# Natural channel order for the second pair's tables, GpSimd costs in the plan, and a new instruction order, in a state-space convolution with an MLP

## The chip, the cores and the metric

The kernel runs on one core of one Trainium2 chip. The metric is device microseconds of one execution of the whole program, less being better. Each engine (TensorE = PE, its weight loads = PEld, VectorE = DVE, ScalarE = ACT, GpSimd = POOL, and SyncE = SP, which issues the DMAs) works through its own instructions in order and waits on semaphores for the others.

## The reference

A pre-norm block over 2048 positions of 512 channels: a diagonal state-space model (S4) as a long convolution, then a channel MLP.

```python
def _A_ref(u, A_re, A_im, B_re, B_im, C_re, C_im, log_dt, Dskip):
    dt = jnp.exp(log_dt)[:, None]
    logdA = dt * (A_re + 1j * A_im)               # 512 x 128
    dB = dt * (B_re + 1j * B_im)
    P = jnp.exp(logdA[:, :, None] * l[None, None, :])
    K = jnp.einsum("dn,dnl,dn->dl", Cc, P, dB).real
    Kf, Uf = rfft of K and u, padded to 4096
    y = irfft(Uf * Kf)[..., :L]
    return y + u * Dskip

def _B_ref(x, w1, b1, w2, b2):
    h = gelu(layernorm(x) @ w1 + b1)              # 512 -> 1376
    return h @ w2 + b2

h = x + _A_ref(layernorm(x), ...)
h2 = h + _B_ref(layernorm(h), ...)
```

## The kernel before

The 512 channels are four blocks c = 0..3 of 128, in two pairs: hf or q = 0 is the first pair (c = 0, 1), 1 the second (c = 2, 3). The kernel K(d, l) of a channel is a product over the 128 states of two tables: A with `NA` = 20 rows and B with `NB` = 33 rows, so that A times B, summed over the states, gives the values at all needed positions l. Each table has a real part and an imaginary part of the complex exponential, so per channel there are two small matmuls that add up.

The stages, in the order of the data:

- *Start.* DMAs bring A, B, C, log_dt (as `raw` and `ldt`) and the input u; TensorE transposes A_re with an identity matrix that GpSimd builds (`ident_fn`, L649); VectorE multiplies it with dt into `th` (the decay rates of the channels). GpSimd also fills field tables with many one-column memsets (`fld_fn` L667, `ca_fn` L719). Splits into a high and a low half and `restack`, many small SBUF-to-SBUF DMAs issued by SyncE (L549), bring rates and phases into the layout in which TensorE multiplies them by positions. ScalarE scales two of the splits (`split`, `CP`, L606); both engines are allowed.
- *Magnitudes.* `bexps` (ScalarE, L774) writes the B tables `EB`, `aexps` (TensorE L985, ScalarE L989 for the first pair and L992 for the second) the A tables `EA` (c = 0, 1) and `EA2` (c = 2, 3).
- *Phases.* `chain(hf, kind)` adds phase steps in PSUM by matmuls (L1033, L1036, L1042), takes a Sin and a Cos of them (ScalarE, L1051, 1024 entries each) into one of three scratch buffers `SC`, and VectorE multiplies the magnitudes by them into imaginary tables (`IA`, `IB`, `IA2`) and real tables in place: with one instruction of 2048 entries (`product`, L1012), or, for the second pair's B tables, with two of 1024 (L1070, L1071).
- *Products.* `kgen(c)` multiplies, channel by channel: 128 channels, four at a time in the four column quarters of the array, each with one matmul of the real tables (L1101) and one of the imaginary (L1102), 20 stationary columns and 33 moving ones. Results are cast from PSUM, Dskip is added to one row (L1115), and `carry` (L1122) moves rows by DMA.
- *Spectrum.* `kspec` (TensorE L1145) transforms K to frequencies in two halves of rows and two blocks; the casts go to SBUF, by DMA to DRAM (`AK_d`) and back in another layout, and `fstage` (L959) does the second step of the transform. `xspec` (L939, L959) does the same for the normalised input (`unorm`, L927, on VectorE or GpSimd; its statistics L915).
- *Back.* `inverse` multiplies the spectra (L1193; VectorE or GpSimd), transforms back (L1209), turns by DMA transposes (L1215); `tail` (L1272 to L1315) adds x, takes the second layer norm, whose reciprocal root GpSimd computes as a power (`root`, L895; VectorE continues at L614), and `mlp` (L1331 to L1355) does the two MLP matmuls, the GELU (L1333) and the residual, and stores.

Casts from PSUM (`evac`) go to ScalarE (L537) or VectorE (L539). PSUM is four buffers of two banks, handed out by the scheduler. L1447 are TensorE instructions without use that fill gaps.

In `chain` and `aexps`, channels of the first pair keep their natural order: entry d of a block at element d of a 128-entry row, so a channel's 20 A entries lie 256 bytes apart. The second pair's A tables are stored by quarter g, row a, channel i (`EA2`, `IA2`: shape (2, 4, 32, 32)), so the 20 entries of a channel lie 64 bytes apart; its B tables hold channel 32g + i at element 4i + g:

```python
if c < 2:
    Ar, Ai = EA[c], IA[c]
    w, x = (lambda v, g, i: v.ap()[:, :, 32 * g + i]), (lambda v, g, i: v.ap()[:, :, 32 * g + i])
else:
    Ar, Ai = EA2[c - 2], IA2[c - 2]
    w, x = (lambda v, g, i: v.ap()[:, g, 0:NA, i]), (lambda v, g, i: v.ap()[:, :, 4 * i + g])
...
pe.matmul(o, lhsT=w(Ar, g, i0 + i), rhs=x(Br, g, i0 + i), start=True, stop=False, tile_position=(0, 32 * g))
pe.matmul(o, lhsT=w(Ai, g, i0 + i), rhs=x(Bi, g, i0 + i), start=False, stop=True, tile_position=(0, 32 * g))
```

All work is a list of 982 steps (`S.add`), each with its engine or engines and a cost in microseconds, and their data dependencies. `ORDER` is a written list of all steps: it sets the order on every engine, the engine where there are two (a negative entry takes the second), and, over a model of the costs (`Sched.run`), which PSUM buffer a step gets and how many filling matmuls go in. A GpSimd step also waits for the VectorE step last issued before it. The model's costs have no other effect on the program.

Of the kernel before, what the change touches and what calls it, by code (L numbers as in the profile page):

```python
# [9 lines left out]
ACT = mybir.ActivationFunctionType  # L10
# [152 lines left out]
class VS(V):  # L163
# [49 lines left out]
]  # L213


FREE = {"PE": 5.0, "ACT": 0.7, "DVE": 0.8, "POOL": 1.4, "SP": 0.7}
WIN, PHASE, ACTIVE = 3.4133, -1.4, 1.25
SWITCH = 0.095


class Clock:
    def __init__(self):
        self.end, self.act, self.warm = PHASE + WIN, 0.0, False

# [184 lines left out]
def kernel(ctx, tc, A_u, A_A_re, A_A_im, A_B_re, A_B_im, A_C_re, A_C_im, A_log_dt, A_Dskip,  # L409
# [64 lines left out]
    EB0 = E0 + 2 * ASZ  # L474
    BA0 = E0 + 2 * ASZ + NCH * BSZ
    IB0 = BA0 + 2 * ASZ
    IA2 = at(BA0 + 2 * ASZ + NCH * BSZ, bf16, 2, 4, 32, 32)
    EA2 = at(IA2.hi, bf16, 2, 4, 32, 32)
    pos[0] = EA2.hi
    HF = 2 * ASZ + 2 * BSZ  # L480
# [1013 lines left out]
```

## Time and profile before

| | us |
|---|---|
| median of 3 runs | 246.31 (246.04 to 247.08) |
| the profiled execution | 247.44 |
| its span, first to last instruction | 245.6 |
| TensorE busy | 208.3 (85%) |
| VectorE busy | 179.9 (73%) |
| ScalarE busy | 182.8 (74%) |
| GpSimd busy | 48.1 (20%) |

The granted TensorE clock was 1.0. In the profile, a row of the timeline gives start and duration in us, engine, line, operation, operands, count, and in brackets how long the engine had been idle and what released it; a row of groups gives busy us, mean ns of one, and idle time before. Busy time of TensorE counts overlapping matmuls once.

### The profile page before, as it was taken

The page shows a single profiled execution, that of the slowest core. Times are in us where ns is not written, and L with a number is a line of the kernel's source. Part 1 is how long each engine was busy: PE and PEld are TensorE (multiplying, and loading weights), DVE is VectorE, ACT ScalarE, POOL GpSimd, SP SyncE. Part 2 cuts the span into 40 slices and gives each one's busy share as a digit, 9 for nine tenths or more (in the row PEclk, how much of TensorE's full clock was granted, in tenths as well). Part 3 has the DMA queues.
Part 4 walks back from the last instruction along what each step waited for, and adds up shares of the span by engine and source line. Part 5 has one row for each costly group of instructions (what it writes and reads, how often), then busy time and mean ns, then how long its engine had stood idle before and what let it go on. Part 6 is the DMA issues. An engine that isn't in the chain of part 4 may idle for free.

```text
span 245.6 us, 7723 instructions
## 1 busy us (share of the span) xinstructions
PE 208.3 (85%) x3268; PEld 116.5 (47%) x3279; DVE 179.9 (73%) x311; ACT 182.8 (74%) x215; POOL 48.1 (20%) x225
## 2 busy tenths in 40 slices
PE   7200788867999999999699898999999999999994
PEld 3200543323776697645576434554444444444452
DVE  0999958899999996489886888999980887031021
ACT  4999998999999987889798979999356214704600
POOL 8834431000000041234604271010000001000000
PEclk9999999999999999999999999999999999999999
DMA  4293250100000160499868958307845053410303
GB/s 150 53 205 76 71 99 17 43 4 3 3 5 5 34 174 7 118 276 275 339 113 155 230 170 286 91 3 138 122 85 109 0 96 86 77 33 21 85 17 79
DMA packets 42755, 24.28 MB, mean 99 GB/s; under 512 B 26145, under 2 KB 40066, under 8 KB 42722
## 3 DMA queue, kind: packets, MB, share of 16 engines
q1 hardware_dynamic: 42130, 23.34, 39.8%
q8 instruction: 25, 0.41, 0.7%
q10 hardware_dynamic: 592, 0.46, 0.6%
q14 instruction: 8, 0.07, 0.1%
HBM read 10.03 MB, written 6.29 MB: 66 GB/s over the span
## 4 chain that ended last, share of the span: by engine, by line
PE 38%; DVE 8%; DMA 4%; ACT 3%; issue 2%; POOL 1%; SPq 0%; DVEq 0%; POOLq 0%
PE ps L1331 15%; PE ps L1353 14%; PE ps L1209 4%; ACT ar L537 3%; DMA AK_d<-ar 2%; DVE ar L1287 2%; DMA ar<-AK_d 2%; PE ps L959 2%; DVE ar L539 1%; PE ps L1277 1%; PE ps L939 1%; DVE ar L1193 1%; POOL ar L895 1%; DVE ar L1284 1%; DVE ar L1198 0%
## 5 line engine op out<-in xcount | busy, mean ns | idle before, releaser
L537 ACT CAST ar<-ps 128x1024 bf16<-128x1024 f32 (+2 forms) x71 | 67.6, 1025 | 15.2 <-DMA ar<-ar 3.5
L1333 ACT ACTIVATE ar<-ps,ar 128x512 bf16<-128x512 f32 (+1 forms) x44 | 29.0, 693 | 25.0 <-PE ps L1331 23.6
L1331 PE MATMUL ps<-ar 128*128 128x512 bf16 (+1 forms) x176 | 39.9, 379 | 0.0
L1353 PE MATMUL ps<-ar 128*128 128x512 bf16 (+3 forms) x181 | 39.2, 366 | 0.6 <-DVE ar L1355 0.3
L1051 ACT ACTIVATE ar<-ps 128x1024 bf16<-128x1024 int16 x36 | 34.6, 1051 | 2.6 <-PE ps L1042 0.9
L1355 DVE TENSOR_TENSOR ar<-ps,ar 128x512 bf16<-128x512 f32 (+1 forms) x17 | 11.0, 656 | 27.8 <-PE ps L1353 20.0
L539 DVE CAST ar<-ps 128x1024 bf16<-128x1024 f32 (+1 forms) x21 | 23.9, 1151 | 5.2 <-PE ps L959 2.8
L1353 PEld LDWEIGHTS <-ar 128*128 128x128 bf16 (+1 forms) x187 | 18.0, 98 | 20.4 <-issue 1.0
L1193 DVE TENSOR_TENSOR ar<-ar 128x2048 bf16<-128x2048 bf16 x22 | 26.5, 1228 | 1.2 <-PE ps L1209 0.9
L1331 PEld LDWEIGHTS <-ar 128*128 128x128 bf16 (+1 forms) x176 | 17.2, 100 | 20.1 <-issue 0.8
L1042 PE MATMUL ps<-ar 128*32 128x512 f16 (+1 forms) x368 | 21.9, 331 | 4.8 <-ACT ar L1051 3.6
L1101 PE MATMUL ps<-ar 128*20 128x33 bf16 x512 | 24.4, 277 | 0.8 <-issue 0.5
L1102 PE MATMUL ps<-ar 128*20 128x33 bf16 x512 | 24.5, 279 | 0.0
L985 PE MATMUL ps<-ar 128*32 128x256 f16 x160 | 7.3, 341 | 19.1 <-DVE ar L722 18.4
L1101 PEld LDWEIGHTS <-ar 128*20 128x20 bf16 x512 | 22.0, 135 | 2.7 <-issue 1.0
L1102 PEld LDWEIGHTS <-ar 128*20 128x20 bf16 x512 | 22.2, 136 | 1.4 <-issue 0.9
L895 POOL TENSOR_TENSOR ar<-ar 128x4 f32<-128x4 f32 (+1 forms) x5 | 5.8, 1165 | 67.6 <-DVE ar L588 44.6
L959 PE MATMUL ps<-ar 128*32 128x256 bf16 (+1 forms) x384 | 17.4, 309 | 1.4 <-DMA ar<-AK_d 1.0
L621 ACT ACTIVATE ar<-ar 128x512 f32<-128x512 f32 (+9 forms) x19 | 16.2, 864 | 3.0 <-DMA ar<-in_A_log_dt_dram 2.9
L1012 DVE TENSOR_TENSOR ar<-ar 128x2048 bf16<-128x2048 bf16 x14 | 16.9, 1219 | 0.3 <-ACT ar L1051 0.2
L939 PE MATMUL ps<-ar 128*32 128x512 bf16 x256 | 16.7, 381 | 0.0
L1042 PEld LDWEIGHTS <-ar 128*32 128x32 f16 x368 | 9.5, 97 | 14.5 <-issue 10.8
(104 smaller groups left out, 305.0 us busy)
## 6 DMA issues: line engine op xcount, KB each, us to landing
AK_d<-ar SPq DMA_DIRECT2D x8, 512.0 KB
ar<-AK_d SPq DMA_DIRECT2D x8, 512.0 KB
ar<-in_A_u_dram SPq DMA_DIRECT2D x4, 512.0 KB
out_dram<-ar SPq DMA_DIRECT2D x30, 64.0 KB
ar<-in_B_w_dram SPq DMA_DIRECT2D x4, 344.0 KB
ar<-ar SPq DMA_DIRECT2D x40, 32.0 KB
ar<-in_B_w_dram SPq DMA_DIRECT2D x2, 640.0 KB
ar<-ar SPq DMA_DIRECT2D x8, 48.0 KB
```

Source lines behind the costliest of these rows:

```text
L537: act.copy(out_fn(), in_fn())
L539: dve.tensor_copy(out_fn(), in_fn())
L939: pe.matmul(pst(p)[32 * cg:32 * cg + 32, 512 * z:512 * z + 512], lhsT=BD.ap()[:, 32 * f + 2 - 2 * jl:32 * f + 34 - 2 * jl], rhs=un[2 * (2 ...
L959: pe.matmul(pst(p)[64 * h + z:64 * h + z + 32, w * (k + r):w * (k + r) + w], lhsT=T.ap()[:, f, r, z:z + 32], rhs=rhs(f), start=True, stop= ...
L1042: pe.matmul(pst(p)[32 * g:32 * g + 32, 256 * j:256 * (j + n)].rearrange("p (a b) -> p a b", a=n), lhsT=W2[DELTAS.index(d)].ap(), rhs=S2[g] ...
L1051: add("ACT", c_act(1024), lambda e, o_=o_, i_=i_: act.activation(o_(), i_(), ACT.Sin, scale=SINSC), r=[p, TBL], w=[sc[cs]])
L1101: pe.matmul(o, lhsT=w(Ar, g, i0 + i), rhs=x(Br, g, i0 + i), start=True, stop=False, tile_position=(0, 32 * g))
L1102: pe.matmul(o, lhsT=w(Ai, g, i0 + i), rhs=x(Bi, g, i0 + i), start=False, stop=True, tile_position=(0, 32 * g))
L1193: (dve if e == "DVE" else gp).tensor_tensor(pieces(o).rearrange("p z (a r d) -> p a z r d", a=4, r=2), k, x, ALU.mult)
L1331: pe.matmul(pst(p)[:fs, 512 * z:512 * z + 512], lhsT=w1s[dc].ap()[:, fc * P:fc * P + fs], rhs=ybuf.ap().rearrange("p (t c) k -> p c t k", ...
L1333: add("ACT", c_act(512, 1), lambda e, p=p, z=z, fc=fc, fs=fs: act.activation(hT.ap()[:fs, fc, :], pst(p)[:fs, 512 * z:512 * z + 512], ACT. ...
L1353: pe.matmul(pst(p)[:, 512 * z + c0:512 * z + c1], lhsT=hT.ap()[:fs, fc, 128 * t:128 * t + 128], rhs=w2s[fc].ap()[:fs, c0:c1], start=(fc == ...
```

## The change

The second pair's tables take the first pair's layout. `th` loses its permuted copy, so three multiplications become one. `EA2` and `IA2` stay where they were and become plain addresses of two tables of 20 x 128 each; `aexps`, `chain` and `kgen` treat both pairs alike. In `chain` the second pair's two B products per group become one `product`, and its A products write rows of 512 entries where they wrote runs of 128. The sines of the second pair's B tables are no longer permuted. The GpSimd costs of `root`, `unorm` and `inverse` in the plan are changed. `ORDER` is new: 976 steps, with 43 on GpSimd (50 before), 310 on VectorE (310), 221 on ScalarE (220), 273 on TensorE (273) and 129 on SyncE (129).

What the new order does, where the prediction speaks of it:

- On GpSimd, the identity follows an iota, the field memsets (`fld_fn`), an iota, `ca_fn` and an iota; before, it was the third step.
- The two scalings of the phase splits (`CP` in `split`) go from ScalarE to VectorE; eight small memsets and three larger steps go from GpSimd to VectorE, and three from VectorE to GpSimd; of the first half's eight `unorm` steps GpSimd takes six (before three, one of which moves to VectorE), and of the second half's eight, six (before eight).
- On SyncE, the four loads of u stand earlier among the `restack` DMAs, one piece of w2 (`w2s[10]`) stands among them, and a bias load goes behind them. After the first pair's carries come three writes to `AK_d`, the two reads of the first of these, and then the second pair's carries.
- On TensorE, the second pair's products hold two `kspec` steps: the first pair's block 0, upper rows, after the first 32 groups of four channels' matmuls, and block 1, upper rows, after 76 of 128.
- On ScalarE, after the last Sin of `chain`: four `kspec` casts, the Sin over 2048 entries (`T`), a `kspec` cast, the table load for the GELU, the first cast of the second pair's products.
- On VectorE, two casts stand between the operand of the 8-entry `root` and the step that reads its result.

```diff
 ORDER = [
...
-    IA2 = at(BA0 + 2 * ASZ + NCH * BSZ, bf16, 2, 4, 32, 32)
-    EA2 = at(IA2.hi, bf16, 2, 4, 32, 32)
-    pos[0] = EA2.hi
+    IA2 = BA0 + 2 * ASZ + NCH * BSZ
+    EA2 = IA2 + 16384
+    pos[0] = EA2 + 16384
...
-    EA = [at(E0 + c * ASZ, bf16, NA, CW) for c in range(2)]
+    EA = [at(lo + c * ASZ, bf16, NA, CW) for lo in (E0, EA2) for c in range(2)]
...
-    IA = [at(BA0 + c * ASZ, bf16, NA, CW) for c in range(2)]
+    IA = [at(lo + c * ASZ, bf16, NA, CW) for lo in (BA0, IA2) for c in range(2)]
...
-    th = tL(f32, 5, 256)
+    th = tL(f32, 4, 256)
     p, pa = tr("are")
-    TT(th[2], p, dtb, ALU.mult, n=256, psum=True, oap=by4(th[2], 0, 256), aap=lambda pa=pa: pa()[:, 0:64], bap=by4(dtb, 0, 256))
-    def th3(e, p=p):
...
-    add("DVE", c_dve(256, 1, True), th3, r=[p, dtb], w=[th[3]], hv=0)
-    TT(th[4], p, dtb, ALU.mult, n=256, psum=True, oap=by4(th[4], 0, 256), aap=lambda pa=pa: pa()[:, 64:128], bap=by4(dtb, 256, 512), pr=0.42)
+    TT(th[2:4], p, dtb, ALU.mult, psum=True, oap=lambda: th[2:4].ap().rearrange("p h d -> p (h d)").rearrange("p (q d) -> p q d", d=4), aap=pa, bap=by4(dtb))
...
-        add("POOL", 0.3, lambda e: gp.tensor_tensor(y.ap(), v_.ap(), mhalf.ap()[:, 0:n], ALU.pow), r=[v_, mhalf], w=[y], hv=6, pr=pr)
+        add("POOL", 0.4 + 0.16 * n, lambda e: gp.tensor_tensor(y.ap(), v_.ap(), mhalf.ap()[:, 0:n], ALU.pow), r=[v_, mhalf], w=[y], hv=6, pr=pr)
...
-            add(("DVE", "POOL"), (c_dve(512, 4) + 0.13, 0.6), ufn, hv=9, r=[hs[8 * b + j], nw[b][3], nw[b][4]], w=[un[j]], pr=pr + 0.001 * (j // 4))
+            add(("DVE", "POOL"), (c_dve(512, 4) + 0.13, 1.15), ufn, hv=9, r=[hs[8 * b + j], nw[b][3], nw[b][4]], w=[un[j]], pr=pr + 0.001 * (j // 4))
...
-                if hf == 0:
-                    add("ACT", c_act(1024), lambda e, p=p, n=n: act.activation(multi(E0 + 4 * n * 256, ASZ, bf16, 2, 4, CW).rearrange("p c a d -> p a c d"), pst(p).rearrange("p (a c d) -> p a c d", a=4, c=2), ACT.Exp),
-                        r=[p, TBL], w=[EA[c][4 * n + z] for c in range(2) for z in range(4)])
-                else:
-                    add("ACT", c_act(1024), lambda e, p=p, n=n: act.activation(dmaj(EA2, 4 * n).rearrange("p x a i -> p a x i"), pst(p).rearrange("p (a x i) -> p a x i", a=4, x=8), ACT.Exp),
-                        r=[p, TBL], w=[EA2])
+                e0 = (E0, EA2)[hf]
+                add("ACT", c_act(1024), lambda e, p=p, n=n, e0=e0: act.activation(multi(e0 + 4 * n * 256, ASZ, bf16, 2, 4, CW).rearrange("p c a d -> p a c d"), pst(p).rearrange("p (a c d) -> p a c d", a=4, c=2), ACT.Exp),
+                    r=[p, TBL], w=[EA[2 * hf + c][4 * n + z] for c in range(2) for z in range(4)])
...
-                if dm:
-                    o_, i_ = (lambda sc=sc, cs=cs: sc[cs].ap().rearrange("p a d -> p (a d)").rearrange("p (x a i) -> p a x i", x=8, a=4)), (lambda p=p: i16v(p).rearrange("p (a x i) -> p a x i", a=4, x=8))
-                elif hf:
-                    o_, i_ = (lambda sc=sc, cs=cs: ced(sc[cs]).rearrange("p c e (i g) -> p e c i g", g=4)), (lambda p=p: i16v(p).rearrange("p (e c g i) -> p e c i g", c=2, g=4, i=32))
-                else:
-                    o_, i_ = (lambda sc=sc, cs=cs: ced(sc[cs]).rearrange("p c e d -> p e c d")), (lambda p=p: i16v(p).rearrange("p (e c d) -> p e c d", e=4, c=2))
+                o_, i_ = (lambda sc=sc, cs=cs: ced(sc[cs]).rearrange("p c e d -> p e c d")), (lambda p=p: i16v(p).rearrange("p (e c d) -> p e c d", e=4, c=2))
...
-            if dm:
-                out = (lambda b0=b0: V(ar, IA2.lo, bf16, (2, 8, 1024)).ap()[:, :, :, 32 * b0:32 * b0 + 128])
-                product(out, lambda o: o[:, 1], sc, [EA2, sc], [IA2, EA2] + mark)
-                continue
...
-                e0, i0, q, lo = E0, BA0, ASZ, b0 * 256
+                e0, i0, q, lo = (E0, EA2)[hf], (BA0, IA2)[hf], ASZ, b0 * 256
             rE, rI = regs(e0, q, lo, 4), regs(i0, q, lo, 4)
-            if hf:
-                add("DVE", c_dve(1024, 2), lambda e, lo=lo, Sx=Sx, e0=e0, i0=i0, q=q: dve.tensor_tensor(ent(i0, q, lo, 4), ent(e0, q, lo, 4), Sx(), ALU.mult), r=rE + [sc[0]], w=rI)
-                add("DVE", c_dve(1024, 2), lambda e, lo=lo, Cx=Cx, e0=e0, q=q: dve.tensor_tensor(ent(e0, q, lo, 4), ent(e0, q, lo, 4), Cx(), ALU.mult), r=rE + [sc[1]], w=rE + mark)
-                continue
             product(lambda e0=e0, q=q, lo=lo: both(e0, q, lo, 4), lambda o: o[:, 1], sc, rE + [sc], rE + rI + mark)
...
-        Br, Bi = EB[c], IB[c]
...
+        Ar, Br, Ai, Bi = EA[c], EB[c], IA[c], IB[c]
...
-                                pe.matmul(o, lhsT=w(Ar, g, i0 + i), rhs=x(Br, g, i0 + i), start=True, stop=False, tile_position=(0, 32 * g))
-                                pe.matmul(o, lhsT=w(Ai, g, i0 + i), rhs=x(Bi, g, i0 + i), start=False, stop=True, tile_position=(0, 32 * g))
+                                pe.matmul(o, lhsT=Ar.ap()[:, :, d], rhs=Br.ap()[:, :, d], start=True, stop=False, tile_position=(0, 32 * g))
+                                pe.matmul(o, lhsT=Ai.ap()[:, :, d], rhs=Bi.ap()[:, :, d], start=False, stop=True, tile_position=(0, 32 * g))
...
-                add(("DVE", "POOL"), (c_dve(2048, 2), 4.85), mul, hv=5, r=[kf[f0:f0 + 8], X.h[f0 // 8][c]], w=o)
+                add(("DVE", "POOL"), (c_dve(2048, 2), 4.0), mul, hv=5, r=[kf[f0:f0 + 8], X.h[f0 // 8][c]], w=o)
```

More of the change, by code (lines that the diff above doesn't have):

```diff
@@ L502 @@
     OB = [[PR[0:2], PR[2:4]], [QR, [at(lo + 24576, bf16, 4, 2, CW) for lo in (E0, BA0)], [at(sc0 + 12288 + 2048 * n, bf16, 4, 2, CW) for n in range(2)]]]
-    Z = [[at(lo, bf16, P, 16) for lo in q] for q in ((zlo, sc0 + 8192), (EA2.lo + 11264, IA2.lo + 11264))]
+    Z = [[at(lo, bf16, P, 16) for lo in q] for q in ((zlo, sc0 + 8192), (EA2 + 11264, IA2 + 11264))]
     assert pos[0] <= NBYTES, pos[0]
-    EA = [at(E0 + c * ASZ, bf16, NA, CW) for c in range(2)]
+    EA = [at(lo + c * ASZ, bf16, NA, CW) for lo in (E0, EA2) for c in range(2)]
     EB = [at(EB0 + c * BSZ, bf16, NB, CW) for c in range(NCH)]
-    IA = [at(BA0 + c * ASZ, bf16, NA, CW) for c in range(2)]
+    IA = [at(lo + c * ASZ, bf16, NA, CW) for lo in (BA0, IA2) for c in range(2)]
     IB = [at(IB0 + c * BSZ, bf16, NB, CW) for c in range(NCH)]
@@ L566 @@
     tE = Tmp(BA0, BA0 + HF)
-    tL = Tmp(BA0 + HF, IA2.hi)
+    tL = Tmp(BA0 + HF, EA2)
     ct = tL
@@ L756, in tr @@
         return p, (lambda: nat(pst(p, bf16)[:, 0:512]))
-    th = tL(f32, 5, 256)
-    thn = lambda: th.ap().rearrange("p h d -> p (h d)").rearrange("p (a q) -> p a q", q=256)[:, 2:5:2, :]
+    th = tL(f32, 4, 256)
     p, pa = tr("are")
-    TT(th[2], p, dtb, ALU.mult, n=256, psum=True, oap=by4(th[2], 0, 256), aap=lambda pa=pa: pa()[:, 0:64], bap=by4(dtb, 0, 256))
-    def th3(e, p=p):
-        for c in range(2):
-            o = th[3].ap().rearrange("p (c e d g) -> p c e d g", c=2, e=8, d=4)[:, c]
-            x = pst(p, bf16)[:, 0:512].rearrange("p (d c g e) -> p c e d g", d=4, c=4, g=4)[:, 2 + c]
-            y = dtb.ap().rearrange("p (c g e d) -> p c e d g", c=4, g=4, e=8)[:, 2 + c]
-            dve.tensor_tensor(o, x, y, ALU.mult)
-    add("DVE", c_dve(256, 1, True), th3, r=[p, dtb], w=[th[3]], hv=0)
-    TT(th[4], p, dtb, ALU.mult, n=256, psum=True, oap=by4(th[4], 0, 256), aap=lambda pa=pa: pa()[:, 64:128], bap=by4(dtb, 256, 512), pr=0.42)
+    TT(th[2:4], p, dtb, ALU.mult, psum=True, oap=lambda: th[2:4].ap().rearrange("p h d -> p (h d)").rearrange("p (q d) -> p q d", d=4), aap=pa, bap=by4(dtb))
     CP(th[0:2], th[2:4], -1.0, n=512, pr=0.35)
@@ L807 @@
     STT(lnd, lnd, 2.0, s1, ALU.mult, ALU.add)
+    thn = lambda: th[2:4].ap().rearrange("p h d -> p (h d)")
     HLt = tL(f16, 2, 512)
@@ L811 @@
     TT(HLg[1], lnd, HLg[0], ALU.subtract, pr=0.41, eng="POOL")
-    TS(HLt[0], th[2:5], 1.0, None, ALU.mult, iap=thn, oap=lambda: HLt[0].ap().rearrange("p (a q) -> p a q", q=256), pr=0.42)
-    STT(HLt[1], th[2:5], 1.0, HLt[0], ALU.mult, ALU.subtract, aap=thn, oap=lambda: HLt[1].ap().rearrange("p (a q) -> p a q", q=256), bap=lambda: HLt[0].ap().rearrange("p (a q) -> p a q", q=256), pr=0.42)
+    TS(HLt[0], th[2:4], 1.0, None, ALU.mult, iap=thn, pr=0.42)
+    STT(HLt[1], th[2:4], 1.0, HLt[0], ALU.mult, ALU.subtract, aap=thn, pr=0.42)
     S3 = tL(f16, 4, 512)
@@ L971, in regs @@
         return [at(lo0 + q * c + lo, bf16, n, CW) for c in range(2)]
-    def dmaj(v, a):
-        return v.ap().rearrange("p c g a i -> p (c g) a i")[:, :, a:a + 4, :]
     def aexps(pr):
@@ L1000, in both @@
     def both(lo0, q, lo, n):
-        k = BA0 - E0
-        a = ar[:, E0 // 2:E0 // 2 + k].rearrange("p (z q) -> p z q", z=2)[:, ::-1, (lo0 - E0) // 2:(lo0 - E0) // 2 + q]
+        if lo0 == EA2:
+            a = ar[:, IA2 // 2:IA2 // 2 + 16384].rearrange("p (z q) -> p z q", z=2)[:, :, 0:q]
+        else:
+            k = BA0 - E0
+            a = ar[:, E0 // 2:E0 // 2 + k].rearrange("p (z q) -> p z q", z=2)[:, ::-1, (lo0 - E0) // 2:(lo0 - E0) // 2 + q]
         return a.rearrange("p z (c q) -> p z c q", c=2)[:, :, :, lo // 2:lo // 2 + n * CW]
@@ L1015, in chain @@
     def chain(hf, kind, pr):
-        dm = hf == 1 and kind == "A"
         ch0 = 256 * hf
@@ L1080, in kgen @@
     def kgen(c, pr):
-        Br, Bi = EB[c], IB[c]
-        if c < 2:
-            Ar, Ai = EA[c], IA[c]
-            w, x = (lambda v, g, i: v.ap()[:, :, 32 * g + i]), (lambda v, g, i: v.ap()[:, :, 32 * g + i])
-        else:
-            Ar, Ai = EA2[c - 2], IA2[c - 2]
-            w, x = (lambda v, g, i: v.ap()[:, g, 0:NA, i]), (lambda v, g, i: v.ap()[:, :, 4 * i + g])
+        Ar, Br, Ai, Bi = EA[c], EB[c], IA[c], IB[c]
         kg = Kg[c // 2]
@@ L1099, in fn @@
                             for g in range(4):
+                                d = 32 * g + i0 + i
                                 o = pst(p)[32 * g:32 * g + NA, 512 * nb:512 * nb + NB * n].rearrange("p (k i) -> p k i", i=n)[:, :, i]
-                                pe.matmul(o, lhsT=w(Ar, g, i0 + i), rhs=x(Br, g, i0 + i), start=True, stop=False, tile_position=(0, 32 * g))
-                                pe.matmul(o, lhsT=w(Ai, g, i0 + i), rhs=x(Bi, g, i0 + i), start=False, stop=True, tile_position=(0, 32 * g))
+                                pe.matmul(o, lhsT=Ar.ap()[:, :, d], rhs=Br.ap()[:, :, d], start=True, stop=False, tile_position=(0, 32 * g))
+                                pe.matmul(o, lhsT=Ai.ap()[:, :, d], rhs=Bi.ap()[:, :, d], start=False, stop=True, tile_position=(0, 32 * g))
                     add("PE", 0.14 * (hi - lo), fn, r=[Ar, Br, Ai, Bi], w=[p], new=[p] if first else [])
@@ L1229 @@
     hT = at(Kg[0].lo, bf16, NFC, 512)
-    w1s = [at(EA2.lo + 2752 * c, bf16, F) for c in range(4)]
-    w2s = [at(IA2.lo + 1024 * fc, bf16, 512) for fc in range(11)]
-    ots = [at(lo, bf16, 512) for lo in [sc0 + 8192 + 1024 * n for n in range(4)] + [EA2.lo + 15360, IA2.lo + 15360, E0, E0 + 1024]]
+    w1s = [at(EA2 + 2752 * c, bf16, F) for c in range(4)]
+    w2s = [at(IA2 + 1024 * fc, bf16, 512) for fc in range(11)]
+    ots = [at(lo, bf16, 512) for lo in [sc0 + 8192 + 1024 * n for n in range(4)] + [EA2 + 15360, IA2 + 15360, E0, E0 + 1024]]
     y2s = [at(PR[2 * n].lo, bf16, 4, 512) for n in range(2)]
```

68 rows, old and new, of the table ORDER are left out of this document.

## The prediction

> **What bounds the kernel now.** I read the page's first lines, then the busy time in stretches of 10 us, then the groups of instructions in single stages, then the timeline and the chain that ended last.
>
> ```profile
> span 245.6 us, 7723 instructions
> PE 208.3 (85%) x3268; PEld 116.5 (47%) x3279; DVE 179.9 (73%) x311; ACT 182.8 (74%) x215; POOL 48.1 (20%) x225
> ```
>
> The shares are means over stages, so they do not say what limits a stage. The stretches do (columns: busy us and instructions of each engine, granted clock, DMA share, GB/s):
>
> ```profile
> core 0: us, PE busy (x) PEld busy (x) DVE busy (x) ACT busy (x) POOL busy (x), PEclk, DMA share, GB/s
> 60.00:70.00 10.00, 9.68 (x347) 7.00 (x344) 9.74 (x20) 10.00 (x12) 0.00 (x0) 1.00 0.02 5
> 70.00:80.00 10.00, 9.32 (x349) 6.89 (x342) 9.81 (x19) 9.04 (x12) 0.20 (x1) 1.00 0.02 5
> 80.00:90.00 10.00, 9.78 (x285) 7.82 (x286) 9.93 (x9) 9.84 (x6) 3.10 (x3) 1.00 0.49 126
> 90.00:100.00 10.00, 9.47 (x313) 8.16 (x306) 6.39 (x14) 7.02 (x6) 1.20 (x1) 1.00 0.02 6
> 100.00:110.00 10.00, 10.00 (x188) 4.46 (x180) 7.62 (x11) 8.46 (x9) 2.96 (x3) 1.00 0.82 224
> 210.00:220.00 10.00, 9.95 (x47) 4.66 (x47) 1.38 (x2) 3.90 (x6) 0.00 (x0) 1.00 0.35 67
> ```
>
> Up to 80 us ScalarE and VectorE are full; there the tables are made. From 80 us TensorE is full or nearly so, and it stays so to the end, so a microsecond of TensorE work taken out at 80 to 100 is worth about a microsecond, if what follows can start earlier too. The instruction counts show the odd place: VectorE does 19 or 20 instructions in each of the two stretches before 80, and 9 in the next, at the same busy time. Instructions have become longer there.
>
> In 62 to 79 us TensorE multiplies the first pair of channel blocks (`kgen` of c = 0, 1), in 82.3 to 99.2 the second pair (c = 2, 3). Both are 256 matmuls on each of the lines L1101 and L1102, of one shape. The first two rows are of the groups in 60 to 80 us, the other two in 80 to 100 (busy us, mean ns of one, idle before):
>
> ```profile
> L1102 PE MATMUL ps<-ar 128*20 128x33 bf16 x256 | 9.9, 249 | 0.0
> L1101 PE MATMUL ps<-ar 128*20 128x33 bf16 x256 | 9.8, 248 | 0.1
> ...
> L1102 PE MATMUL ps<-ar 128*20 128x33 bf16 x256 | 14.6, 309 | 0.0
> L1101 PE MATMUL ps<-ar 128*20 128x33 bf16 x256 | 14.5, 305 | 0.8 <-issue 0.5 <-DVE ar L1012 0.2
> ```
>
> The same work takes 4.7 us more. The pace in the timeline, groups of four matmuls in the four column quarters, L1101 and L1102 by turns (start, us, engine, line):
>
> ```profile
> 64.15 0.26 PE L1101 MATMUL ps<-ar 128*20 128x33 bf16 x4
> ...
> 65.10 0.27 PE L1101 MATMUL ps<-ar 128*20 128x33 bf16 x4
> ...
> 93.30 0.34 PE L1101 MATMUL ps<-ar 128*20 128x33 bf16 x4
> ...
> 94.63 0.33 PE L1101 MATMUL ps<-ar 128*20 128x33 bf16 x4
> ```
>
> Between each two rows shown lie 14 groups: 0.95 us in the first pair, 0.068 a group; 1.33 us in the second, 0.095. At 93 to 95 us the DMA share is near nothing (row 90 to 100: 0.02). What differs between the pairs in code is the layout: of the second pair `w` takes the 20 stationary columns 64 bytes apart (first pair 256) and the four quarters' moving entries lie side by side (first pair 64 bytes apart).
>
> Other engines are slow beside it too:
>
> ```profile
> 44.84 1.05 ACT L621 ACTIVATE ar<-ar 128x1024 bf16<-128x1024 int16 x1
> ...
> 63.25 1.14 ACT L621 ACTIVATE ar<-ar 128x1024 bf16<-128x1024 int16 x1
> ...
> 82.15 2.47 ACT L537 CAST ar<-ps 128x1024 bf16<-128x1024 f32 x1 [0.16 <-PE ps L1145]
> ...
> 84.53 0.95 ACT L537 CAST ar<-ps 128x1024 bf16<-128x1024 f32 x1
> ...
> 85.38 5.50 ACT L621 ACTIVATE ar<-ar 128x2048 bf16<-128x2048 int16 x1
> ...
> 26.00 0.68 DVE L915 BATCH_NORM_STATS2 ar<-ar 128x6 f32<-128x512 bf16 x1
> ...
> 86.78 1.65 DVE L915 BATCH_NORM_STATS2 ar<-ar 128x6 f32<-128x512 bf16 x1
> ```
>
> A Sin over 1024 entries takes 1.05 alone and 1.14 beside the first pair's products; one over 2048 takes 5.50 beside the second's, where twice 1.05 is 2.1. One cast takes 2.47, another 0.95. The statistics take 1.65 for 0.68.
>
> **The path behind.** The second pair's products set off the chain that ends last:
>
> ```profile
> 99.88 0.18 DVE L1115 TENSOR_TENSOR ar<-ar 128x32 bf16<-128x32 bf16 x1 [2.12 <-ACT ar L537]
> ...
> 100.08 3.48 SPq L1122 DMA_DIRECT2D ar<-ar  x4
> ...
> 108.54 5.22 DMA AK_d<-ar
> ...
> 113.85 4.74 DMA ar<-AK_d
> ...
> 235.37 6.57 PE ps L1353 x35
> ```
>
> When the last product is cast and Dskip added (99.88), the carries go out (100.08), the spectrum is made, written to DRAM (5.22) and read back (4.74), and so on to the last MLP matmuls. So both the TensorE work and the chain's start move with the end of the products.
>
> **The change, part by part.**
>
> *The second pair's layout* (`aexps`, `chain`, `kgen`): exponentials, sines and products of c = 2, 3 are written as those of c = 0, 1. I price the second pair's matmuls by the first pair's rows: 14.5 - 9.8 = 4.7 us less. Bounds: the pace alone gives (0.095 - 0.068) x 128 groups = 3.5; the whole 14.5 against 128 x 0.068 = 8.7 gives 5.8. I take 4.7, the difference of like rows, and all of it on the path: TensorE waits for almost nothing in 82 to 99. The new order puts a wait in (the last rival works it out: 1.4 us), against which the gap of 0.5 us before L1101 and the larger bound stand. ScalarE's exponentials and sines keep their count and sizes: nothing.
>
> [...]
>
> *VectorE's merged products*: four pairs of products become four single ones.
>
> ```profile
> L1070 DVE TENSOR_TENSOR ar<-ar 128x1024 bf16<-128x1024 bf16 x4 | 2.8, 693 | 0.1
> L1071 DVE TENSOR_TENSOR ar<-ar 128x1024 bf16<-128x1024 bf16 x4 | 2.8, 689 | 0.0
> L1012 DVE TENSOR_TENSOR ar<-ar 128x2048 bf16<-128x2048 bf16 x14 | 16.9, 1219 | 0.3 <-ACT ar L1051 0.2
> L1051 ACT ACTIVATE ar<-ps 128x1024 bf16<-128x1024 int16 x19 | 18.5, 1061 | 1.0 <-DVE ar L1071 0.5 <-DVE ar L1115 0.5
> ```
>
> Each pair costs 0.693 + 0.689 and becomes 1.219: 0.16 less, 0.65 for four. The last row (60 to 80 us) shows what of it ends a wait: the sines waited 0.5 us for L1071. I take 0.3 of a possible 0 to 0.65.
>
> *The start.* The three products of A_re with dt become one, but in the new order GpSimd builds the identity matrix that the transposes need behind the field memsets (L667), three iotas and the `ca` memsets:
>
> ```profile
> 1.74 0.29 POOL L649 TENSOR_SCALAR_AFFINE_SELECT ar<-ar 128x128 bf16<-128x128 bf16 x1
> 2.99 2.30 POOL L667 MEMSET ar<- 128x1 int32 x68
> 4.92 0.34 PEld L754 LDWEIGHTS <-ar 128*128 128x128 bf16 x4 [0.84 <-DMA ar<-in_A_A_re_dram]
> ...
> L606 ACT ACTIVATE ar<-ar 128x512 f16<-128x512 f32 x2 | 1.2, 616 | 0.0
> ...
> 38.70 0.61 PE L1042 MATMUL ps<-ar 128*32 128x256 f16 x13 [0.36 <-DMA ar<-ar]
> ```
>
> Today it stands at 2.03 and the transposes wait for the data until 4.92. The 2.30 of L667 ahead of it alone put it at 4.3, the iotas and the `ca` memsets (small, not shown) past 4.92, so the start may be some tenths late; the two scalings that move from ScalarE to VectorE (L606, 0.62 each) give 1.2 back to the engine that is full. But the first sines wait for TensorE, and TensorE at 38.70 for the last of the little restacking DMAs, which SyncE issues one by one. Before the last of these stand as many DMAs as now (one weight load more, one bias load less). So I take 0, with 0.9 either way. Other instructions go from GpSimd to VectorE and back; what they add to VectorE lies before 40 us, beside that DMA wait.
>
> *GpSimd's durations* are numbers of the plan alone. They act through the order:
>
> ```profile
> DVE ar L614 <- POOL ar L895: 4.6, 4, 1.8
> ```
>
> Four times VectorE waits for GpSimd's power, 4.6 us in all, the longest 1.8, just ahead of the casts that feed the transfer at 108.54. In the new order two casts (of `kspec` and `xspec`) stand between that power's operand and its first user; they cover it. I take 1.0 (0 to 1.8), since such casts wait for TensorE as well. The rest of the new order after 105 us moves casts between two engines that both have room; I price it at 0.
>
> *Sum*: 4.7 + 0.3 + 0 + 1.0 = 6.0 us. The profiled execution took 247.44 us for its span of 245.6, and the median of the runs is 246.31. So the span should be near 239.6, that execution 241.4 and the median **240.3**. The ends: 5.8 + 0.65 + 0.9 + 1.8 = 9.2 gives 237.1; 3.5 - 0.9 = 2.6 gives 243.7.
>
> **The rivals.**
>
> *The layout is not the cause.* The second pair's A tables lie elsewhere (`EA2`, `IA2`, 16 KB apart), and statistics and the long Sin run beside them; the place and the company stay. Then the first term is 0 and 0.3 + 1.0 remain: **245.0**. For it: the cast at 84.53 ran beside the same products in 0.95, and nothing in the code says why 64 bytes should be worse than 256. Against it: at 93.3 to 94.6 the slow pace stands with the long Sin long over, and the first pair kept its pace beside two full engines. [...] The trace does not settle it: most that runs beside the second pair is slow, and the cast at 84.53 is not.
>
> *The contention stays, and the new order exposes it: slower.* In the new order ScalarE does, from about 81.0: four spectrum casts, the long Sin, a cast, a table load, and the first product's cast, which frees a PSUM buffer. TensorE needs it for a K-spectrum step placed behind 76 of the 128 groups.
>
> ```profile
> L531 ACT ACT_TABLE_LOAD x3 | 3.8, 1283 | 0.8 <-PEq L1478 0.7
> ```
>
> Unstretched that queue is 4 x 0.95 + 2.1 + 0.95 + 1.28 + 0.77 = 8.9 us, to 89.9 (0.77 is the smaller cast, an estimate from 0.95 by its size); TensorE arrives at 82.3 + 76 x 0.068 + about 1 for another spectrum step = 88.5 and waits 1.4. If the stretched Sin and cast stay (5.50 and 2.47, 4.9 us more), the buffer comes free at 94.8, while at the old pace (14.5 / 128 = 0.113) TensorE arrives at 91.9: a wait of 2.9. Less the 1.3 gained elsewhere that is 1.6 slower: **247.9**. It decides from a stretch of 3.3 us on.
>
> **How the numbers follow.** A difference under 0.5% (1.2 us: 245.1 to 247.5) cannot be told from none here. Forecast 0.80, no cause in layout 0.12, exposed contention 0.08. Faster by over 0.5%: nearly all of the forecast and half of the second, 0.78 + 0.06 = 0.84; the same: 0.02 + 0.05 = 0.07; slower: 0.08 + 0.01 = 0.09. The forecast's own ends are 237.1 and 243.7; to leave out no more than 2 in 10 the range reaches to the second case: 237.1 to 245.2.
>
> **What would show it.** Right: the second pair's rows of the two matmul lines near 9.8 us busy and 250 ns, 0.068 a group; the 2048-entry Sin near 2.1; no statistics over 0.8; the carries of the second pair before 96 us. The merged products show as 18 of the 2048-entry kind. The GpSimd term is right if VectorE's wait for the 8-entry power is under 0.8. Wrong: the second pair's products still at 14 us, which kills the first term; or the products fast but TensorE with new waits of several us between 82 and 155, which would mean that the gain went into the queues behind.

## The result and the profile after

The changed kernel takes 256.02 us (median of 4 runs, 253.95 to 258.92) where the kernel before took 246.69 in the runs beside it: a ratio of 1.035 (95% interval 1.026 to 1.044). Ratios here and below leave out runs in which the chip was disturbed; medians do not. The profiled execution took 255.03 us for its span of 253.2.

Read the same views as before. The first lines, then the stretches:

```profile
span 253.2 us, 7753 instructions
PE 209.9 (83%) x3293; PEld 113.2 (45%) x3293; DVE 172.3 (68%) x310; ACT 178.0 (70%) x216; POOL 41.2 (16%) x218
```

VectorE and ScalarE are less busy than before (172.3 and 178.0 us; before 179.9 and 182.8), TensorE about as busy (209.9, before 208.3), and the span is 7.6 us longer. So hardly anything has become costlier; somebody waits.

```profile
60.00:70.00 10.00, 5.38 (x176) 3.72 (x168) 8.18 (x15) 6.91 (x9) 0.00 (x0) 1.00 0.01 3
70.00:80.00 10.00, 7.40 (x234) 5.53 (x238) 4.31 (x9) 5.34 (x6) 0.00 (x0) 0.66 0.01 2
80.00:90.00 10.00, 8.97 (x304) 6.42 (x299) 7.94 (x12) 9.01 (x12) 0.00 (x0) 1.00 0.05 10
90.00:100.00 10.00, 7.49 (x331) 5.75 (x323) 7.74 (x12) 8.26 (x8) 3.91 (x6) 1.00 0.74 174
100.00:110.00 10.00, 7.27 (x272) 5.31 (x276) 1.52 (x8) 3.54 (x5) 1.67 (x1) 0.83 0.40 121
```

Two places lose time. In 60 to 80, where three engines were full before, TensorE falls to 5.38 and 7.40, VectorE to 4.31, ScalarE to 5.34 in the second stretch: all three idle at once, so they wait for one another. In 90 to 110 TensorE falls to 7.5 and 7.3 where it was 9.5 and 10.0. The granted clock of TensorE reads 0.66 and 0.83 in two of the stretches in which it idles or has just idled. From 210 on TensorE is full, as before.

The first place, by the waits in 60 to 110 us (who waited for whom: us in total, times, longest) and three rows of the timeline:

```profile
PE ps L1071 <- DVE ar L1000: 7.9, 4, 2.4
DVE ar L1000 <- ACT ar L1033: 5.0, 5, 3.0
DVE ar L1000 <- PE ps L1071: 4.1, 1, 4.1
```

```profile
65.23 0.25 PE L1071 MATMUL ps<-ar 128*20 128x33 bf16 x1 [2.29 <-DVE ar L1000]
...
70.16 0.25 PE L1071 MATMUL ps<-ar 128*20 128x33 bf16 x1 [2.37 <-DVE ar L1000]
...
81.37 1.23 DVE L1000 TENSOR_TENSOR ar<-ar 128x2048 bf16<-128x2048 bf16 x1 [4.06 <-PE ps L1071]
```

L1070 and L1071 are the real and the imaginary matmul of `kgen` in the new numbering, L1000 is `product`, L1033 the Sin of `chain`. Between 62 and 88 us TensorE multiplies the *first* pair while VectorE's products belong to the *second* pair: the two have no data in common. Yet TensorE waits for VectorE four times, as often as there are merged B products, and once VectorE waits 4.06 us for TensorE. VectorE's 5.0 us for the Sin look like the same loss once more, since the Sin's arguments stand on TensorE behind the loads that wait. And it is always the imaginary line that waits, although the real one comes first in each group.

The second place is the second pair itself (groups of 90.5 to 106.5 us, then the pace, then the rows with its idle times):

```profile
L1071 PE MATMUL ps<-ar 128*20 128x33 bf16 x256 | 9.6, 249 | 2.9 <-issue 2.9
L1070 PE MATMUL ps<-ar 128*20 128x33 bf16 x256 | 9.5, 250 | 0.2 <-DVE ar L1000 0.2
```

```profile
95.77 0.32 PE L1070 MATMUL ps<-ar 128*20 128x33 bf16 x4
...
97.66 0.31 PE L1070 MATMUL ps<-ar 128*20 128x33 bf16 x4
```

```profile
95.76 0.25 PE L1071 MATMUL ps<-ar 128*20 128x33 bf16 x1 [0.40 <-issue]
...
100.59 0.24 PE L1071 MATMUL ps<-ar 128*20 128x33 bf16 x1 [2.48 <-issue]
...
109.14 0.83 PE L930 MATMUL ps<-ar 128*32 128x512 bf16 x12 [2.14 <-issue]
```

The pace is what was forecast: 28 groups in 1.89 us, 0.068 each, 249 ns a matmul. But TensorE stops for 2.48 and 2.14 us, each time in the middle of a run of like instructions and with nothing to wait for ("issue"). How many instructions lie between the stops is in the counts of two windows (matmuls and weight loads are the two counts ahead of VectorE's):

```profile
95.74:99.50 3.76, 2.35 (x128) 2.17 (x128) 2.00 (x4) 2.52 (x3) 3.08 (x5) 1.00 1.03 286
100.40:107.05 6.65, 6.41 (x256) 4.99 (x256) 0.82 (x4) 2.40 (x4) 0.00 (x0) 0.74 0.49 163
```

256 instructions from the first stop (0.40 us) to the second, 512 from the second to the third. I read such a regular count as a matter of the supply of instructions, not of data; no row says so. The first 256 were used up in 2.35 us, with the DMA share at 1.03; ahead of the third stop it was lower (0.49 in the second window).

The rest of what was to be seen: the Sin of 2048 entries takes 2.04 us, the statistics 0.68 (5.0 us for 8), the second pair's carries leave at 107.11 (100.08 before).

```profile
93.26 2.04 ACT L621 ACTIVATE ar<-ar 128x2048 bf16<-128x2048 int16 x1
...
107.11 1.54 SPq L1091 DMA_DIRECT2D ar<-ar  x2
```

```profile
L906 DVE BATCH_NORM_STATS2 ar<-ar 128x6 f32<-128x512 bf16 x8 | 5.0, 679 | 0.0
```

### The profile page after: what moved, and what is told of

Read it like the earlier page. It is cut to its first block, busy times and chain, and to the rows that moved or that the text cites. A ratio compares the mean times of both kernels' runs of the same rounds, so it can differ in the third digit from the quotient of the medians.

```text
span 253.2 us, 7753 instructions
## 1 busy us (share of the span) xinstructions
PE 209.9 (83%) x3293; PEld 113.2 (45%) x3293; DVE 172.3 (68%) x310; ACT 178.0 (70%) x216; POOL 41.2 (16%) x218
## 4 chain that ended last, share of the span: by engine, by line
PE 51%; ACT 7%; DVE 5%; issue 4%; DMA 2%; DVEq 0%; ACTq 0%; SPq 0%
PE ps L1300 15%; PE ps L1322 15%; ACT ar L537 5%; PE ps L930 4%; PE ps L950 3%; PE ps L1071 3%; PE ps L1070 3%; PE ps L1246 2%; DMA ar<-ar 2%; PE ps L1114 2%; DVE ar L1000 2%; PE ps L1178 2%; DVE ar L539 1%; ACT ar L1271 1%; DVE ar L1162 1%
## 5 line engine op out<-in xcount | busy, mean ns | idle before, releaser
L537 ACT CAST ar<-ps 128x1024 bf16<-128x1024 f32 (+3 forms) x73 | 66.4, 987 | 18.8 <-PE ps L1114 5.3
L1033 ACT ACTIVATE ar<-ps 128x1024 bf16<-128x1024 int16 x36 | 34.5, 1041 | 8.5 <-PE ps L1029 5.1
L539 DVE CAST ar<-ps 128x1024 bf16<-128x1024 f32 (+1 forms) x19 | 21.4, 1144 | 14.7 <-PE ps L1071 8.1
L1071 PE MATMUL ps<-ar 128*20 128x33 bf16 x512 | 20.4, 249 | 10.8 <-DVE ar L1000 7.9
L1000 DVE TENSOR_TENSOR ar<-ar 128x2048 bf16<-128x2048 bf16 x18 | 21.8, 1221 | 9.3 <-ACT ar L1033 5.0
L1162 DVE TENSOR_TENSOR ar<-ar 128x2048 bf16<-128x2048 bf16 x22 | 26.2, 1220 | 2.1 <-PE ps L1178 1.5
L1416 PE MATMUL ps<-ar 128*128 128x512 bf16 x54 | 16.9, 440 | 12.9 <-DMA ar<-in_A_u_dram 12.4
L1029 PE MATMUL ps<-ar 128*32 128x512 f16 (+1 forms) x368 | 22.9, 342 | 4.7 <-ACT ar L1033 3.4
L1071 PEld LDWEIGHTS <-ar 128*20 128x20 bf16 x512 | 18.0, 125 | 12.7 <-DVE ar L1000 9.3
L1070 PE MATMUL ps<-ar 128*20 128x33 bf16 x512 | 20.8, 249 | 0.2 <-DVE ar L1000 0.2
L950 PE MATMUL ps<-ar 128*32 128x256 bf16 (+1 forms) x384 | 18.1, 309 | 2.0 <-ACT ar L537 1.7
L1070 PEld LDWEIGHTS <-ar 128*20 128x20 bf16 x512 | 18.3, 124 | 2.5 <-issue 1.2
L930 PE MATMUL ps<-ar 128*32 128x512 bf16 x256 | 16.6, 381 | 2.4 <-issue 2.1
L1029 PEld LDWEIGHTS <-ar 128*32 128x32 f16 x368 | 10.3, 99 | 14.3 <-issue 10.7
L598 DVE TENSOR_TENSOR ar<-ar 128x4 f32<-128x4 f32 (+9 forms) x41 | 13.3, 337 | 4.7 <-POOL ar L667 4.0
```

What stands on the lines that cost most here:

```text
L537: act.copy(out_fn(), in_fn())
L930: pe.matmul(pst(p)[32 * cg:32 * cg + 32, 512 * z:512 * z + 512], lhsT=BD.ap()[:, 32 * f + 2 - 2 * jl:32 * f + 34 - 2 * jl], rhs=un[2 * (2 ...
L950: pe.matmul(pst(p)[64 * h + z:64 * h + z + 32, w * (k + r):w * (k + r) + w], lhsT=T.ap()[:, f, r, z:z + 32], rhs=rhs(f), start=True, stop= ...
L1000: dve.tensor_tensor(o, E_(o).unsqueeze(1).to_broadcast(shape), f, ALU.mult)
L1029: pe.matmul(pst(p)[32 * g:32 * g + 32, 256 * j:256 * (j + n)].rearrange("p (a b) -> p a b", a=n), lhsT=W2[DELTAS.index(d)].ap(), rhs=S2[g] ...
L1033: add("ACT", c_act(1024), lambda e, o_=o_, i_=i_: act.activation(o_(), i_(), ACT.Sin, scale=SINSC), r=[p, TBL], w=[sc[cs]])
```

## The experiments

**Theory A (footprint)**: `both` lets one VectorE instruction write an imaginary and a real table. In memory stand, in this order, the real tables (A of the first pair, then B of all four blocks), then the imaginary ones (A of the first pair, then B). From the first to the last address, the merged B product of the second pair therefore spans the imaginary tables of the first pair, A and B, but not the real ones. If the waits are put in for the whole span, TensorE's imaginary matmuls and their weight loads wait for VectorE's products, and VectorE for them. **Theory B (order)**: the waits are a lock step of the new order.

**`split`**: each of the four B products of the second pair as two instructions, in place. The step keeps its place, its cost in the plan and the tables that it names as read and written, so the order and the plan stay what they were.

```diff
+            if hf and kind == "B":
+                def two(e, lo=lo, Sx=Sx, Cx=Cx, e0=e0, i0=i0, q=q):
+                    dve.tensor_tensor(ent(i0, q, lo, 4), ent(e0, q, lo, 4), Sx(), ALU.mult)
+                    dve.tensor_tensor(ent(e0, q, lo, 4), ent(e0, q, lo, 4), Cx(), ALU.mult)
+                add("DVE", c_dve(2048, 2), two, r=rE + [sc], w=rE + rI + mark)
+                continue
             product(lambda e0=e0, q=q, lo=lo: both(e0, q, lo, 4), ...)
```

> The changed kernel, but the second pair's four B products are written again as two instructions of 1024 entries, imaginary table, then real table, where the change has one that spans both; order and layout stay. Theory A (footprint): the one instruction covers, from its first to its last address, the first pair's imaginary A tables, which lie between its two outputs, so TensorE's loads of those tables wait for VectorE and VectorE's next product waits for TensorE. Then TensorE's waits for the products (7.9 us) fall below 1, VectorE's wait of 4.1 for the first pair's matmuls goes, and the span falls by 7 to 10 to 243 to 246 us (time 245 to 248). Theory B (order): the first pair's products stand between the sines' arguments in a lock step that the new order makes, however the product is written; the waits stay and the span is 253 to 254, four times 0.16 us longer if anything.

Measured: 0.998 of the kernel before (0.994 to 1.003), span 245.0, 8.2 us less than the changed kernel. TensorE's waits in 60 to 110 us are now these; nobody waits for the B products, no VectorE wait for the first pair's matmuls is left, and VectorE's waits for the Sin are down from 5.0 us to 0.6 (L1076 and L1077 are `kgen`'s lines here; the 0.4 is the second pair's own last product):

```profile
PE ps L1077 <- issue: 3.0, 1, 3.0
PE ps L930 <- issue: 2.1, 1, 2.1
PE ps L1029 <- ACT ar L1033: 1.1, 3, 0.6
...
PE ps L1076 <- DVE ar L1000: 0.4, 1, 0.4
```

Theory B is out: the order is the same. The stops of 3.0 and 2.1 us ("issue") stay.

**`old_order`** and **`old_order_split`**: the changed kernel with the 976 steps in the order of the kernel before (the six that are gone left out); the second with the split products as well.

> The changed kernel (layout, merged products) with the order of the kernel before, less the six steps that no longer exist. Theory A: waits of TensorE's imaginary loads for VectorE come here too, at two places in the first pair (where a B product of the second pair stands ahead of them in program order); the time lies above what the layout alone would give, 245 to 251 us. Theory B: the waits belong to the new order; here there are none, and the time is what was forecast for the layout, 240 to 242.

> The layout alone: the changed kernel with the order of before and the second pair's B products in two instructions. If the second pair's matmuls were worth what was forecast (4.7 us, all on the path): 241 to 242.5. If they run faster but TensorE then stands still in the middle of a group, waiting for nothing that the profile shows (2.5 and 2.1 us in the changed kernel, while a transfer of instructions is under way): 244 to 246, with such idle times of 2 us or more in the second pair. If the layout is worth nothing: 246 to 247.

Measured: `old_order` 1.020 (1.012 to 1.027), `old_order_split` 1.000 (0.997 to 1.003). The merged product costs 2.0% in the old order too, where its waits are (60 to 100 us):

```profile
PE ps L1078 <- DVE ar L1007: 3.7, 2, 3.4
...
DVE ar L1007 <- PE ps L1078: 6.8, 2, 3.6
```

In the new order the same edit makes 3.7% (1.035 to 0.998). So the merged product is the loss, in either order, and again the line that waits (L1078) is the imaginary one.

`old_order` lost more than expected (252.89 us; 245 to 251 was). `old_order_split` is the layout alone, and by its time, 247.31 against 247.27 us, the layout is worth nothing, the last of the three cases. But its second pair does end earlier, and TensorE's longest stop in it is 1.2 us, not the 2 or more of the middle case (the timeline):

```profile
87.15 0.24 PE L1084 MATMUL ps<-ar 128*20 128x33 bf16 x1 [1.19 <-issue]
...
87.39 1.47 PE L1429 MATMUL ps<-ar 128*128 128x512 bf16 x6
...
97.67 3.48 SPq L1104 DMA_DIRECT2D ar<-ar  x4
...
111.79 0.80 SPq L556 DMA_DIRECT2D ar<-AK_d  x2
...
117.30 2.76 PE L1429 MATMUL ps<-ar 128*128 128x512 bf16 x12
...
120.00 1.96 PE L1191 MATMUL ps<-ar 64*128 64x128 bf16 x64
```

The carries leave 2.4 us earlier than before (100.08), the spectrum's read 2.1 earlier (113.85). Then 12 matmuls of L1429 take 2.76 us, and the inverse transform's matmuls (L1191), which began at 119.19 before, begin at 120.00. L1429 is no work: it is the dummy matmul with which the plan fills idle time that it expects of TensorE, and here it expected idle time that was not there. Six more of them, 1.47 us, stand inside the second pair (87.39), where the kernel before has one of 0.39.

**`old_order_split_nofill`** and two controls: no dummy matmuls after 100 us, in the layout with the old order, in the kernel before, and in `split`. Nothing else changes in the programs built from these kernels: every other instruction that uses PSUM keeps its place and its buffer.

```diff
-            if e == "PE" and self.src <= seen and s - free[e] > 0.4 and fs:
+            if e == "PE" and self.src <= seen and s - free[e] > 0.4 and fs and s < 100.0:
```

> The layout alone (order of before, B products in two), without the dummy matmuls that the plan puts into TensorE's expected idle times after 100 us (24 records between 100 and 150 us, 12 of them, 2.7 us, in one place ahead of the inverse transform's matmuls). If the layout's lead of 2.2 us at the spectrum's read is lost to them: 244 to 245.5 us, faster than before by 0.7 to 1%. If the lead is lost for another reason (TensorE has as much work and the next operand is late anyway): 246.5 to 247.5.

> The kernel before the change, without the dummy matmuls that the plan puts into TensorE's expected idle times after 100 us (5 records between 100 and 150 us, 10 after that). If the gain of 1.1% that the layout with the old order showed without them is the layout's lead set free: here 0 to -0.3% (ratio 0.997 to 1.000). If the dummy matmuls cost the kernel before as much: ratio near 0.989, and the layout is worth nothing after all.

> The changed kernel with the B products in two instructions and without the dummy matmuls after 100 us (7 records between 100 and 150 us, 8 after). Few of them stand on the path here, so if the new order is as good as the old one: 245 to 247.5, a ratio to the kernel before of 0.99 to 1.00, level with the same edit in the old order (0.989) at best, since TensorE's stops of 3.0 and 2.1 us for instructions stay.

Measured: 0.989 (0.985 to 0.992), 1.0045 (1.0016 to 1.0075) and 1.0096 (1.006 to 1.013). In the first, the inverse transform follows the spectrum's matmuls without a gap:

```profile
115.82 0.62 PE L957 MATMUL ps<-ar 128*32 128x256 bf16 x16 [0.98 <-DMA ar<-AK_d]
116.37 1.96 PE L1191 MATMUL ps<-ar 64*128 64x128 bf16 x64
```

That is 2.8 us before the kernel before (119.19), and 1.1% of 247.92 us is 2.8. The kernel before gains nothing by the same edit: it loses 0.45%, where 0 to 0.3% of gain was the one forecast and 1.1% the other. So the gain is the layout's, set free. `split` loses too (1.0096, where 0.99 to 1.00 was expected); why these two kernels are faster with the dummy matmuls than without is open. `old_order_split_nofill` beats both kernels.

**What made the second pair slow**: `w64` and `xadj`, both from `split`, change one side of the second pair's reads each.

```diff
 w64:   w = lambda v, d: V(ar, v.lo, bf16, (4, NA, 32)).ap()[:, d // 32, :, d % 32]     # stationary
 xadj:  x = lambda v, d: v.ap()[:, :, 4 * (d % 32) + d // 32]                           # moving
```

> The split kernel, but the second pair's stationary columns are read 64 bytes apart (first pair 256) from the same tables, which changes which entries are multiplied; the moving entries stay 64 bytes apart. If the stationary step makes the slow pace of before, the second pair's two matmul lines show about 300 ns of mean and 0.095 us a group, and work beside them is stretched (the Sin of 2048 entries 4 us or more for 2.0); if the moving side makes it, they stay at 249 ns and 0.068.

> The split kernel, but of the second pair's moving tables the four column quarters read entries that lie side by side (2 bytes apart, as before the change; here 64), which changes which entries are multiplied; the stationary columns stay 256 bytes apart. The 64-byte stationary step alone left the pace at 252 ns. If the moving entries' place makes the slow pace: the second pair's matmuls near 300 ns, 0.095 us a group, the Sin of 2048 entries 4 us or more, statistics over 1 us. If neither side alone does: 250 ns, and the cause of the slow pace is the two together or the tables' place.

Measured (groups in 80 to 115 us; in `w64` 20 matmuls of the first pair are among them), two rows of `w64`; in the second block four of `xadj`; in the third the Sin of `split`:

```profile
L1080 PE MATMUL ps<-ar 128*20 128x33 bf16 x276 | 11.1, 254 | 2.7 <-issue 2.6
L1079 PE MATMUL ps<-ar 128*20 128x33 bf16 x276 | 11.0, 255 | 0.4 <-issue 0.4
```

```profile
L1078 PE MATMUL ps<-ar 128*20 128x33 bf16 x256 | 14.5, 311 | 0.0
L1077 PE MATMUL ps<-ar 128*20 128x33 bf16 x256 | 14.5, 306 | 1.6 <-ACT ar L537 1.3 <-DVE ar L1000 0.4
L621 ACT ACTIVATE ar<-ar 128x2048 bf16<-128x2048 int16 x1 | 4.2, 4216 | 0.0
L906 DVE BATCH_NORM_STATS2 ar<-ar 128x6 f32<-128x512 bf16 x8 | 8.7, 1139 | 0.0
```

```profile
L621 ACT ACTIVATE ar<-ar 128x2048 bf16<-128x2048 int16 x1 | 2.0, 1981 | 0.0
```

The 64-byte step of the stationary columns does next to nothing (254 ns for 249). The moving entries of the four column quarters, 2 bytes apart instead of 64, bring the slow pace back in full: 14.5 us, 306 to 311 ns. They bring back most of what was slow beside it: the Sin takes 4.2 us for 2.0 (5.50 in the kernel before), the statistics 1.14 for 0.68 (1.40 on average before). What in the reading of such entries is slow, no run shows. Each of the two kernels ran once, so their times (253.67 and 252.34 us) are not used.

**The stops of TensorE**: `split_late` moves five transfers of the first pair's spectrum, and the two matmul steps that use them with their casts, behind the second pair's carries.

> The split kernel, with the first pair's three writes of K's spectrum to DRAM, their two reads and the two steps that use them put behind the second pair's carries in the order, so that no large transfer runs beside the second pair's products. TensorE stood still for 3.0 us in them, waiting for nothing the profile shows, 256 instructions after the last such stop. If the DMA load makes the instruction transfers late, the stops shrink to 1.2 or less each and the second pair takes 2 us less; if 256 instructions in 2.35 us are too many for the supply by themselves, stops of 2.5 to 3 remain. The span is no measure here: the spectrum's transfers come 8 us later, so 246 to 255 us.

Measured (one run, 259.02 us where 246 to 255 was expected; the spectrum is late): two stops of 0.6 us where there were 3.0 and 2.1, and the second pair's carries leave at 96.98, in `split` at 99.49. Waits and timeline of `split_late`, then the row of `split`:

```profile
PE ps L1084 <- issue: 0.6, 1, 0.6
PE ps L937 <- issue: 0.6, 1, 0.6
```

```profile
96.98 3.32 SPq L1104 DMA_DIRECT2D ar<-ar  x4
```

```profile
99.49 0.77 SPq L1097 DMA_DIRECT2D ar<-ar  x1
```

So the long stops belong to large transfers beside TensorE's products. The profile also records the transfers of instructions, packets of 16 KB on a queue of their own (q8; 25 of them, 0.41 MB, in the changed kernel). In `split_late` these are alone in 88 to 97 us, three of them, and the row of GB/s (40 slices of 0.225 us) shows when they start:

```profile
GB/s 73 0 0 0 0 0 0 0 0 0 0 0 0 0 0 73 0 0 0 0 0 0 0 0 0 0 0 0 0 0 0 73 0 0 0 0 0 0 0 0
...
q8 instruction: 3, 0.05, 2.0%
```

They start at 88.12, 91.56 and 95.08, 3.4 to 3.5 us apart. Beside the large transfers the two ahead of the long stop start 4.9 us apart in the changed kernel (93.42, 98.29) and 5.5 in `split` (85.23, 90.71). In each of these three kernels a packet takes 0.9 to 1.0 us, and TensorE goes on 1.2 to 1.5 us after the one that, by the times, it stood still for has landed (in the changed kernel at 99.17 and 107.87; on at 100.59 and 109.14). So a packet is not slower beside other transfers; it starts later. In the kernel before, two start 5.5 us apart as well (84.71, 90.24), but at the old pace only 0.5 us of that showed as a stop. How late a packet starts does not follow from the DMA share alone: `old_order_split` stopped for 1.2 us (on at 87.15) beside shares of 0.86 and 0.98 (84 to 86, 86 to 88), `split` for 3.0 beside 1.03 (88 to 92). The pace matters too: `xadj`, with the order of `split` and the slow pace (306 to 311 ns), has no such stop on the lines of the second pair's products; one of 0.8 us is left, on L930.

## Why the prediction was wrong

*The step that failed* is "VectorE's merged products": "four pairs of products become four single ones", priced at -0.3 us, 0 to 0.65. The whole forecast was -6.0 us and +9.3 was measured (256.02 against 246.69). The instructions did become 18 of 1.22 us. But I counted only their durations, and an instruction that writes two tables far apart also changes who must wait for it. That was 3.7% of the time, 9 us, in the new order and 2.0%, 5 us, in the old. What is left without it (`split`, 0.998) is no gain either, though 5.7 us of gain were forecast for the other terms; what is known of them stands below. It could have been asked of the code: which tables lie between the two outputs, and who reads them meanwhile? `both` was in the kernel before, but there the first pair's products are all done before `kgen` starts. That the waits come from the span of addresses follows from the table order, from the imaginary line alone waiting, and from `split`. The instruction lists of the programs built from the kernels show the waits themselves: in the changed kernel four weight loads of the first pair's imaginary A tables wait for a merged product of the second pair, which writes on both sides of these tables and nothing in them. In `old_order` there are two, as many as in its trace; in `split`, `old_order_split` and the kernel before there is none.

*The layout's pace* (-4.7): right as a pace, wrong as a gain. 14.5 us became 9.6 and 0.068 a group came as said. What reaches the path is 2.4 us at the carries (`old_order_split`), and 2.8 at the end only without the dummy matmuls after 100 us. Of the 2.3 us missing at the carries, the stops make about 1.1 (1.6 us, before 0.5) and the dummy matmuls inside the second pair another 1.1 (1.47, before 0.39). The first missing piece is the instruction supply: "TensorE waits for almost nothing in 82 to 99" held for the old pace, at which 256 instructions (32 groups of 0.113) lasted 3.6 us; at 0.068 they last 2.2 and, as I read the stops, the supply becomes the bound: the packets above came 3.4 to 5.5 us apart. The code could have hinted at it: in both kernels the plan's model (`Sched.run`) can hold TensorE back at every 256th instruction, longer while transfers are pending. The second piece is that a stage that ends earlier is worth nothing if the plan has put dummy work behind it. The wait of 1.4 us for a PSUM buffer, which the prediction charged to this term, does not show: in 88 to 110 us TensorE of the changed kernel waits for no cast.

*What I named as the difference*, stationary columns 64 bytes apart or moving entries side by side, is now decided for the moving side: the stationary step alone left 254 ns for 249 (`w64`), the place of the moving entries alone made 306 to 311 (`xadj`). The Sin beside them says the same: only the moving entries' place differs between one of 1.98 us (`split`) and one of 4.2 (`xadj`).

*The start* (0 ± 0.9): right. VectorE waited 4.0 us for GpSimd's memsets (L667), and still the first Sin of `chain` began at 39.93 instead of 40.45 (VectorE's waits for GpSimd after; the Sin after; the Sin before):

```profile
DVE ar L598 <- POOL ar L667: 4.0, 1, 4.0
DVE ar L614 <- POOL ar L886: 2.2, 2, 1.1
```

```profile
39.93 1.02 ACT L1033 ACTIVATE ar<-ps 128x1024 bf16<-128x1024 int16 x1 [0.45 <-PE ps L1029]
```

```profile
40.45 1.02 ACT L1051 ACTIVATE ar<-ps 128x1024 bf16<-128x1024 int16 x1 [0.94 <-PE ps L1042]
```

*GpSimd's power* (-1.0): the wait for the 8-entry power, 1.8 us, is gone as said, and 2.2 of the 4.6 us are left, two waits of 1.1 for 4-entry ones. But `split` and `old_order_split` are level (0.998 and 1.000), so the new order as a whole brings nothing that can be measured; what this term is worth by itself, no run shows.

*The rivals*: "The layout is not the cause" falls (249 ns). "The contention stays" falls too (Sin 2.04); that the kernel became slower, as it said, was luck, for the reason was one that it did not name.

## What to carry to other kernels

Before two writes are merged into one instruction, look at what lies between their outputs: all who read or write there may have to wait for it, however unlike their data (here 3.7% of the time, in the old order 2.0%). A faster stretch of TensorE must be fed: count instructions per microsecond beside bytes, above all while large transfers run (here 256 were used up in 2.35 us at a DMA share of 1.03, and a stop of 2.48 us followed). And when a stage becomes earlier, look at what the plan has put behind it, since filling that was free may now stand on the path (here 12 dummy matmuls, 2.76 us).

## What the runs showed of the hardware

In the changed kernel TensorE stopped after exactly 256 and 512 instructions, for 2.48 us behind a stretch with a DMA share of 1.03 and for 2.14 behind one of 0.49. The longest stop was 3.0 us in `split`, beside a share of 1.03 (88 to 92 us), and 0.6 in `split_late`, where in 88 to 97 us only three packets of q8 moved (2.0% of the DMA engines' time). No row names such a packet as the releaser; that it is one is inferred from the times (on 1.2 to 1.5 us after landing, three kernels).

Four column quarters that read moving entries 2 bytes apart ran at 306 to 311 ns a matmul instead of 249 at 64 bytes. Beside them ScalarE's Sin took 4.2 us for 2.0 and VectorE's statistics 1.14 for 0.68 (one run, `xadj`).
